# Which weight tiles the second stage decodes in which unit: three and then one, or two throughout

## Chip, cores and metric

The kernel runs on one core of a Trainium2 chip. The metric is the device time of one execution in microseconds (us). TensorE is called PE, VectorE DVE, ScalarE ACT, GpSimd POOL and SyncE SP here, as the profile calls them.

## What is computed

An attention layer, then two feed-forward layers over its 2304 rows of 512 values. The feed-forward weights are float64. The kernel splits each of their values, and the rows themselves, into a high and a low part in the float32 format, so that a product takes three matmuls (high by high, low by high, high by low).

```python
x = attention_with_memory(q, k, v, M_prev, z_prev, beta)   # (2304, 512)
h = x @ w_in                                               # 512 -> 2048
x = (h * tanh(softplus(h))) @ w_out                        # 2048 -> 512
a, b = x @ w1, x @ w2                                      # 512 -> 1024 each
out = ((a * b) @ w3) @ w_out2                              # 1024 -> 1024 -> 512
```

## The kernel before

**Stage one** is the attention, 16 pairs of heads. **Stage two** is the first feed-forward layer, and the change lies there. It takes the 2048 hidden columns in four quarters (`g`), and within a quarter eight units: four blocks of rows (`b`) by two halves of 288 rows (`z`). A unit runs 48 matmuls of `emit_h` (x by a quarter of `w_in`) and 48 of `emit_x2` (the activated result by a quarter of `w_out`), the latter for the unit before. `emit_x2` sums into PSUM banks of the tag X, of which there are three, and for each of its four column blocks DVE adds the bank to `x2` in SBUF (L575 in the first quarter, L577 later), which frees the bank for the block three further on. **The last stage** holds the second feed-forward layer; its `fold`, begun during the last quarter, multiplies `w3` by `w_out2` beforehand.

**Decoding.** A weight tile of 128x512 float64 values is turned into float32 pairs by `decode`: one load of 512 KB on SP's queue (L92), six DVE instructions (L98 to L104) and an addition on POOL (L105). Then one of two things follows:

- `split_w`, for the next quarter's weights (the generator `load_quarter(g + 1)`, eight tiles, called `nextq` in the loop): POOL rounds (L62) and subtracts (L65) into the tile `wqt`, and that is all. Such a tile is called N here.
- `split_to_dram`, for the weights of the last stage (the generator `predecode`, 24 tiles of `w1`, `w2` and `w_out2`, called `pre`): POOL rounds (L62) and subtracts (L120) in place, and two stores of 256 KB go out on SP's queue (L121, L122) to DRAM, from where the last stage reads them. Such a tile is called P here.

Both use the same buffers: `decoder(dk, 2, 2)` gives two for the raw load (`draw`) and two each for `da` and `de`. The next tile in a pair of `da` and `de` begins when POOL has subtracted, for an N, and when the stores have landed, for a P. Two P tiles are decoded during stage one, so 22 are left for stage two. The quarter after the present one needs its eight N tiles at its own start.

**What sets the order.** Each engine runs its instructions in a fixed order. A planner writes it when the program is built (`schedule_with_timeline_sim`): it takes an instruction of lower place in the source early when its own estimate of times says that the engine would be idle and the buffers are free. So where a step stands in the source is not just where it runs; once the order is written, an instruction that waits holds up all that stand behind it on its engine.

The loop of stage two, before: every unit asks for two steps of `nextq` (which has eight, so it is done after four units) and one step of `pre`.

Of the kernel before, what the change touches and what calls it, by code (L numbers as in the profile page):

```python
# [21 lines left out]
def fused_kernel(ctx: ExitStack, tc, q, k, v, M_prev, z_prev, beta, w_in, w_out, w1, w2, w3, w_out2, out):  # L22
# [47 lines left out]
    def steps(gen, n):  # L70

        for _ in range(n):
            next(gen, None)
# [9 lines left out]
    def decoder(stack, raw, n):  # L83
        dec.update(pool=stack.enter_context(tc.tile_pool(name="dec", bufs=1)), raw=raw, n=n)
# [54 lines left out]
    def predecode():  # L139
        for w, wd in ((w1, w1_dram), (w2, w2_dram), (w_out2, o2_dram)):  # L140
            for c in range(w.shape[0] // 128):
                for h in range(w.shape[1] // WN):
                    split_to_dram(wd[:, 128 * c:128 * c + 128, WN * h:WN * h + WN], words(w, 128 * c, WN * h))
                    yield
# [13 lines left out]
    def load_quarter(g):  # L158
        t = (wq if g % 2 == 0 else w2q[0]).tile([128, 2, KD + KQ, FQ], F32R, tag=f"wq{g % 2}", name="wqt")
        wts[g] = t  # L160
        for c in range(KD):
            split_w(t[:, 0, c], t[:, 1, c], words(w_in, 128 * c, FQ * g))
            yield
        for c in range(KQ):
            split_w(t[:, 0, KD + c], t[:, 1, KD + c], words(w_out, FQ * g + 128 * c, 0))
            yield
# [287 lines left out]
    def emit_h(u):  # L454

        g, b, z = u
        t = wts[g]
        x = xl[b]
        cs = slice(CH * z, CH * z + CH)
        y = [wps[0].tile([128, 2, CH], F32, tag=f"y{i}", name="y", bufs=1) for i in range(2)]  # L460
        hp = []
        for m in range(KQ):
            o = bank(HU.get(u, HT[g == NQ - 1])[m])[:, 0:CH]
            ms = slice(128 * m, 128 * m + 128)
            for kk in range(KD):
                mm(o, t[:, 0, kk, ms], x[:, 0, kk, cs], kk == 0, False)
                mm(o, t[:, 0, kk, ms], x[:, 1, kk, cs], False, False)
                mm(o, t[:, 1, kk, ms], x[:, 0, kk, cs], False, kk == KD - 1)
            hp.append(o)
        for m in range(KQ):  # L470
            nc.scalar.activation(out=y[m // 2][:, m % 2], in_=hp[m], func=AF.Tanh, scale=0.5)

        d = wps[0].tile([128, 1], F32, tag="dum", name="dum", bufs=2)
        first = nc.scalar.activation(out=d, in_=y[1][:, 1, 0:1], func=AF.Sin, scale=0.0)
        with tc.issue_after(first.ins):
            for i in range(2):
                nc.scalar.activation(out=y[i], in_=y[i], func=AF.Arctan, scale=-0.5, bias=half)
        gg = []
        for i in range(2):
            nc.scalar.activation(out=y[i], in_=y[i], func=AF.Sin, scale=-2.0, bias=halfpi)  # L480
            for j in range(2):
                nc.vector.tensor_tensor(out=y[i][:, j], in0=y[i][:, j], in1=hp[2 * i + j], op=ALU.mult)
            gh = wps[0].tile([128, 2, CH], F32R, tag="gh", name="gh", bufs=3)
            gl = wps[0].tile([128, 2, CH], F32R, tag="gl", name="gl", bufs=3)
            nc.scalar.copy(out=gh, in_=y[i])
            sub(gl, y[i], gh)
            gg.append((gh, gl))
        gt[u] = gg
# [9 lines left out]
    pre = predecode()  # L498
# [61 lines left out]
    def emit_x2(u):  # L560
        g, b, z = u
        t = wts[g]
        gg = gt.pop(u)
        c0 = S * b + CH * z
        for m in range(KD):
            o = psX()[:, 0:CH]
            ms = slice(128 * m, 128 * m + 128)
            for kk in range(KQ):
                gh, gl = (x[:, kk % 2] for x in gg[kk // 2])
                mm(o, t[:, 0, KD + kk, ms], gh, kk == 0, False)  # L570
                mm(o, t[:, 1, KD + kk, ms], gh, False, False)
                mm(o, t[:, 0, KD + kk, ms], gl, False, kk == KQ - 1)
            d = x2[:, m, c0:c0 + CH]
            if g == 0:
                nc.vector.tensor_copy(out=d, in_=o)  # L575
            else:
                nc.vector.tensor_tensor(out=d, in0=d, in1=o, op=ALU.add)  # L577
# [37 lines left out]
    def from_dram(t, d, cols):  # L615
        for i in range(2):
            dm(out=f(t[:, i]), in_=d[i, :, cols].rearrange("(k p) f -> p k f", p=128))

    def w_slot(s, name):
        return xp.tile([128, 2, KD, 512], F32R, tag=f"xs{s}", name=name, padded_shape=[128, 2, KD, S])  # L620

    folding = fold()
    nextq = iter(())
    prev = None
    w1t, w2t, wft = [None, None], [None, None], [None]
    for u in [(g, b, z) for g in range(NQ) for b in range(B) for z in range(2)]:
        g, b, z = u
        last = g == NQ - 1
        if u not in gt:
            if last and fpool[0] is None:  # L630
                steps(nextq, 100)
                steps(pre, 100)
                dk.close()
                fpool[0] = fk.enter_context(tc.tile_pool(name="fp", bufs=1))
                decoder(fk, 1, 2)
            emit_h(u)
        if last:
            if z == 0 and b > 0:
                wt, wd = ((w1t, w1_dram), (w2t, w2_dram))[(b - 1) % 2]
                i = (b - 1) // 2  # L640
                wt[i] = w_slot(b - 1, "w12t")
                from_dram(wt[i], wd, slice(512 * i, 512 * i + 512))
            if b > 0:
                steps(folding, 3)
        if prev is not None:
            emit_x2(prev)
        if not last:
            if b == 0 and z == 0:
                nextq = load_quarter(g + 1)
            steps(nextq, 2)  # L650
            steps(pre, 1)
        prev = u
    emit_x2(prev)
    w2t[1] = w_slot(3, "w12t")
# [101 lines left out]
```

## Time and profile before

| what | us |
|---|---|
| median of 3 runs (1074.55 to 1075.28) | 1075.14 |
| the profiled execution: its own time | 1075.49 |
| the profiled execution: span from first to last instruction | 1073.7 |
| PE busy | 1023.7 |
| DVE busy | 671.9 |
| POOL busy | 387.3 |

A busy time adds up the time in which an engine had an instruction running. For PE the ends are modelled and instructions overlap, so a busy PE need not be at its peak. Times of rows are counted from the start of the span.

### The profile page before, as it was taken

The page shows a single profiled execution, that of the slowest core. Times are in us where ns is not written, and L with a number is a line of the kernel's source. Part 1 is how long each engine was busy: PE and PEld are TensorE (multiplying, and loading weights), DVE is VectorE, ACT ScalarE, POOL GpSimd, SP SyncE. Part 2 cuts the span into 40 slices and gives each one's busy share as a digit, 9 for nine tenths or more (in the row PEclk, how much of TensorE's full clock was granted, in tenths as well). Part 3 has the DMA queues.
Part 4 walks back from the last instruction along what each step waited for, and adds up shares of the span by engine and source line. Part 5 has one row for each costly group of instructions (what it writes and reads, how often), then busy time and mean ns, then how long its engine had stood idle before and what let it go on. Part 6 is the DMA issues. An engine that isn't in the chain of part 4 may idle for free.

```text
span 1073.7 us, 19071 instructions
## 1 busy us (share of the span) xinstructions
PE 1023.7 (95%) x7128; PEld 913.2 (85%) x7128; DVE 671.9 (63%) x1563; ACT 548.0 (51%) x1157; POOL 387.3 (36%) x377
## 2 busy tenths in 40 slices
PE   6998898899998999999999999999999999999998
PEld 5665655567798999999999999999998999999997
DVE  6699999896689888888987535647551122222220
ACT  5776767677765666666666655653231222222221
POOL 7668898784255556555555001010100000000000
PEclk9999999999999999999999999999999999999999
DMA  6788777675233343333332264323115100000001
GB/s 149 167 188 188 186 181 184 169 187 117 79 98 101 112 161 109 109 130 127 118 99 101 63 243 146 136 89 128 62 58 176 40 5 17 20 21 16 6 20 40
DMA packets 111341, 116.70 MB, mean 109 GB/s; under 512 B 71696, under 2 KB 73744, under 8 KB 111248
## 3 DMA queue, kind: packets, MB, share of 16 engines
q1 hardware_dynamic: 111248, 115.48, 37.6%
q8 instruction: 56, 0.92, 0.4%
q14 instruction: 37, 0.30, 0.1%
HBM read 71.83 MB, written 21.50 MB: 87 GB/s over the span
## 4 chain that ended last, share of the span: by engine, by line
PE 62%; DVE 20%; POOL 7%; DMA 6%; issue 3%; SPq 1%; ACT 0%; DVEq 0%; POOLq 0%; ACTq 0%
PE psA L59 28%; PE psX L59 24%; PE psF L59 6%; DVE de L104 3%; POOL da L120 2%; DVE da L102 2%; PE psF L426 2%; DVE de L103 2%; DVE s L361 2%; DVE da L99 2%; POOL da L105 2%; DVE da L98 2%; DVE da L100 2%; DMA w_dram<-da 1%; DVE s L356 1%
## 5 line engine op out<-in xcount | busy, mean ns | idle before, releaser
L105 POOL TENSOR_TENSOR da<-da,de 128x512 f32<-128x512 f32 x72 | 100.1, 1395 | 336.0 <-DVE de L104 272.6
L59 PE MATMUL psX<-gh,wqt 128*128 128x288 f32 x1024 | 209.0, 298 | 9.9 <-DVE x L575 5.4
L59 PE MATMUL psA<-x2h,w12t 128*128 128x256 f32 x1152 | 210.4, 283 | 0.0
L59 PEld LDWEIGHTS psA<-x2h,w12t 128*128 128x128 f32 x1152 | 180.8, 192 | 1.0
L59 PEld LDWEIGHTS psX<-gh,wqt 128*128 128x128 f32 x1024 | 164.6, 188 | 13.5 <-DVE x L575 6.7
L59 PE MATMUL psA<-x2l,w12t 128*128 128x256 f32 x576 | 163.2, 284 | 0.4 <-DVE x2l L65 0.4
L59 PE MATMUL psX<-gl,wqt 128*128 128x288 f32 x512 | 150.9, 295 | 0.0
L686 DVE TENSOR_TENSOR bs<-bs,psA 128x256 f32<-128x256 f32 x72 | 30.3, 421 | 161.5 <-PE psA L59 156.8
L59 PE MATMUL psA<-xt,wqt 128*128 128x288 f32 x840 | 119.9, 296 | 0.0
L59 PEld LDWEIGHTS psA<-xt,wqt 128*128 128x128 f32 x840 | 115.0, 189 | 2.3 <-issue 1.0
L59 PEld LDWEIGHTS psA<-x2l,w12t 128*128 128x128 f32 x576 | 110.3, 192 | 1.4 <-DVE x2l L65 0.7
L366 ACT ACTIVATE s<-s,acc 128x512 f32<-128x512 f32 (+4 forms) x144 | 84.2, 587 | 39.7 <-DVE acc L361 34.2
L59 PE MATMUL psX<-wft,pbuf 128*128 128x512 f32 x432 | 101.7, 394 | 2.3 <-DMA wft<-w_dram 2.3
L59 PEld LDWEIGHTS psX<-wft,pbuf 128*128 128x128 f32 x432 | 81.4, 190 | 19.3 <-DMA wft<-w_dram 2.8
L59 PEld LDWEIGHTS psX<-gl,wqt 128*128 128x128 f32 x512 | 96.5, 189 | 0.2
L687 ACT CAST pbuf<-bs 128x256 fp32r<-128x256 f32 x72 | 29.3, 406 | 110.4 <-DVE bs L686 97.3
L98 DVE TENSOR_SCALAR da<-draw 128x512 int32<-128x512 int32 x72 | 44.1, 616 | 61.5 <-DMA draw<-in_moe_w_dram 23.1
L59 PE MATMUL psF<-xt,wqt 128*128 128x288 f32 x552 | 77.3, 295 | 0.0
L426 PE MATMUL psF<-ident,s 128*128 128x128 f32 x400 | 67.7, 283 | 10.0 <-DVE s L356 6.6
L59 PE MATMUL psX<-pt,raw 128*64 128x64 f32 (+4 forms) x576 | 74.8, 329 | 0.0
L59 PEld LDWEIGHTS psF<-xt,wqt 128*128 128x128 f32 x552 | 74.5, 188 | 0.1
L361 DVE CUSTOM_DVE_ANT_0 s<-psA,mask 128x512 f32<-128x512 f32 (+3 forms) x144 | 64.2, 477 | 15.0 <-PE psA L59 11.0
(116 smaller groups left out, 1920.8 us busy)
## 6 DMA issues: line engine op xcount, KB each, us to landing
draw<-in_moe_w_dram SPq DMA_DIRECT2D x32, 512.0 KB, 3.7
draw<-in_moe_w_out_dram SPq DMA_DIRECT2D x24, 512.0 KB, 3.9
draw<-in_moe_w_in_dram SPq DMA_DIRECT2D x16, 512.0 KB, 4.4
w12t<-w_dram SPq DMA_DIRECT2D x8, 1024.0 KB, 7.8
w_dram<-de SPq DMA_DIRECT2D x24, 256.0 KB, 2.4
w_dram<-da SPq DMA_DIRECT2D x24, 256.0 KB, 2.4
out_dram<-ob SPq DMA_DIRECT2D x18, 256.0 KB, 2.0
eqk<-hl SPq DMA_DIRECT2D x30, 144.0 KB, 2.7
```

Source lines behind the costliest of these rows:

```text
L59: nc.tensor.matmul(o, lhsT=l, rhs=r, start=start, stop=stop)
L98: V.tensor_scalar(out=ai, in0=hw, scalar1=0x7FFFFFFF, scalar2=None, op0=ALU.bitwise_and)
L99: V.tensor_scalar(out=a, in0=a, scalar1=2.0 ** -15, scalar2=122879.9921875, op0=ALU.max, op1=ALU.min)
L100: V.tensor_scalar(out=ai, in0=ai, scalar1=3, scalar2=0x3FFFFFF8, op0=ALU.logical_shift_left, op1=ALU.bitwise_and)
L102: V.scalar_tensor_tensor(out=ai, in0=hw, scalar=-0x40000000, in1=ai, op0=ALU.bitwise_and, op1=ALU.bitwise_or)
L104: V.scalar_tensor_tensor(out=e, in0=lw.bitcast(U32), scalar=2.0 ** -52, in1=e, op0=ALU.mult, op1=ALU.mult)
L105: nc.gpsimd.tensor_tensor(out=a, in0=a, in1=e, op=ALU.add)
L361: nc.vector.tensor_tensor_reduce(out=s, in0=o, in1=m, op0=ALU.add, op1=ALU.min, scale=-scale, scalar=init, accum_out=a,)
L366: nc.scalar.activation(out=s, in_=s, func=AF.Exp, scale=-1.0, bias=a, accum_out=r)
L426: nc.tensor.transpose(o[:, 128 * x:128 * x + 128], src[:, 128 * jb:128 * jb + 128], ident)
L686: nc.vector.tensor_tensor(out=bs, in0=bs, in1=pa, op=ALU.mult)
L687: nc.scalar.copy(out=t[:, 0, m], in_=bs)
```

## The change

In the first four units of a quarter (`b` is 0 or 1) the loop asks for two steps of `nextq` and none of `pre`; in the other four for two of `pre`. The 100 in place of the 2 takes whatever is left of `nextq` there, which is nothing. The number of tiles and the instructions of each stay the same; the 22 P tiles are asked for by the unit (2,3,0), the seventh of the third quarter, where it was the sixth.

```diff
         if not last:
             if b == 0 and z == 0:
                 nextq = load_quarter(g + 1)
-            steps(nextq, 2)
-            steps(pre, 1)
+            first_half = b < 2
+            steps(nextq, 2 if first_half else 100)
+            steps(pre, 0 if first_half else 2)
         prev = u
```

## Rows read from the trace of the kernel before

**Rows 1.** The page: busy time of PE and DVE; the chain that ended last.

```profile
PE 1023.7 (95%) x7128; PEld 913.2 (85%) x7128; DVE 671.9 (63%) x1563; ACT 548.0 (51%) x1157; POOL 387.3 (36%) x377
PE 62%; DVE 20%; POOL 7%; DMA 6%; issue 3%; SPq 1%; ACT 0%; DVEq 0%; POOLq 0%; ACTq 0%
```

**Rows 2.** Windows over the first three quarters: stretch, length, then each engine's busy time.

```profile
305.44:398.70 93.26, 88.52 (x659) 87.66 (x660) 81.71 (x154) 59.12 (x93) 49.37 (x42) 1.00 0.37 122
399.25:503.48 104.23, 103.02 (x768) 102.15 (x768) 89.90 (x176) 67.19 (x104) 57.70 (x49) 1.00 0.36 122
503.64:606.00 102.36, 99.30 (x730) 98.60 (x731) 82.64 (x163) 62.61 (x97) 51.93 (x44) 0.98 0.32 104
```

**Rows 3.** Timeline of PE: start, length, instruction, [idle before, releaser].

```profile
330.86 0.54 PE L59 MATMUL psX<-gh,wqt 128*128 128x288 f32 x2 [0.84 <-DVE x L575]
345.84 0.54 PE L59 MATMUL psX<-gh,wqt 128*128 128x288 f32 x2 [2.30 <-DVE x L575]
373.21 0.53 PE L59 MATMUL psX<-gh,wqt 128*128 128x288 f32 x2 [1.59 <-DVE x L575]
477.51 0.54 PE L59 MATMUL psX<-gh,wqt 128*128 128x288 f32 x2 [1.15 <-DVE x L577]
503.64 0.54 PE L59 MATMUL psX<-gh,wqt 128*128 128x288 f32 x2 [0.16 <-DVE x L577]
581.70 0.54 PE L59 MATMUL psX<-gh,wqt 128*128 128x288 f32 x2 [0.91 <-DVE x L577]
596.81 0.53 PE L59 MATMUL psX<-gh,wqt 128*128 128x288 f32 x2 [2.06 <-DVE x L577]
```

**Rows 4.** Windows of line 98 alone, a half quarter each: DVE busy (count).

```profile
399.25:451.40 52.15, 6.30 (x8) 1.00 0.34 112
451.40:503.50 52.10, 4.48 (x8) 1.00 0.39 132
```

**Rows 5.** The chain that ended last, in order of time: start, length, piece.

```profile
468.49 2.78 DMA w_dram<-da
...
482.21 2.00 DMA w_dram<-da
...
496.26 1.99 DMA o_dram<-da
```

**Rows 6.** Timeline of DVE, second quarter: start, length, instruction.

```profile
437.37 0.44 DVE L577 TENSOR_TENSOR x<-x,psX 128x288 f32<-128x288 f32 x1
...
449.90 0.44 DVE L577 TENSOR_TENSOR x<-x,psX 128x288 f32<-128x288 f32 x1
...
461.78 0.45 DVE L577 TENSOR_TENSOR x<-x,psX 128x288 f32<-128x288 f32 x1
...
474.67 1.41 DVE L103 TENSOR_SCALAR de<-da 128x512 int32<-128x512 int32 x1
...
477.02 0.44 DVE L577 TENSOR_TENSOR x<-x,psX 128x288 f32<-128x288 f32 x1
...
490.00 0.44 DVE L577 TENSOR_TENSOR x<-x,psX 128x288 f32<-128x288 f32 x1
...
501.26 0.76 DVE L103 TENSOR_SCALAR de<-da 128x512 int32<-128x512 int32 x2
...
503.13 0.45 DVE L577 TENSOR_TENSOR x<-x,psX 128x288 f32<-128x288 f32 x1
```

**Rows 7.** Timeline of DVE at the start of the first and of the second quarter.

```profile
304.94 0.44 DVE L575 COPY x<-psX 128x288 f32<-128x288 f32 x1
...
310.85 0.43 DVE L98 TENSOR_SCALAR da<-draw 128x512 int32<-128x512 int32 x1 [1.43 <-DMA w_dram<-da]
...
323.57 1.51 DVE L98 TENSOR_SCALAR da<-draw 128x512 int32<-128x512 int32 x1
...
411.61 0.44 DVE L577 TENSOR_TENSOR x<-x,psX 128x288 f32<-128x288 f32 x1
...
428.44 1.49 DVE L98 TENSOR_SCALAR da<-draw 128x512 int32<-128x512 int32 x1 [0.84 <-POOL wqt L65]
```

**Rows 8.** Windows around the start of the last quarter: the share before DMA is the granted clock.

```profile
597.00:600.00 3.00, 3.00 (x16) 3.00 (x16) 1.58 (x5) 1.35 (x2) 0.80 (x1) 0.60 0.56 175
600.00:603.00 3.00, 3.00 (x21) 3.00 (x21) 2.92 (x7) 1.70 (x2) 0.00 (x0) 0.84 0.00 0
603.00:606.00 3.00, 3.00 (x25) 3.00 (x25) 2.06 (x4) 0.82 (x2) 0.76 (x1) 1.00 0.01 3
```

## Prediction

> **What bounds the kernel now.** I read the page first. PE is busy for 95% of the span, yet only 62% of the chain that ended last is PE; 20% is DVE, 7% POOL and 6% DMA [rows 1]. So somewhere PE waits for a loop through those three. I then cut stage two into quarters. PE idles 4.7 us of the first (93.26 less 88.52), 1.2 us of the second and 3.1 us of the third [rows 2]; the second, least disturbed quarter gives PE's own price of a unit, 103.02 / 8 = 12.88 us. All the change can give back is in those 9 us, under 1% of the time.
>
> The timeline of PE shows where they are [rows 3]. Each stall is of one kind: the matmul that needs a bank of tag X waits for DVE's addition to `x2`. That addition depends on nothing slow; it stands behind a pair of decodes in DVE's fixed order, and the decodes are late. Two stalls, 0.84 and 2.30 us, fall in the third and fourth unit of the first quarter. One falls in the sixth unit of every quarter: 1.59, 1.15 and 0.91 us. A tail of 0.16 us follows two units later in the second quarter. The last, 2.06 us, stands at the end of the third quarter, where `w3` is loaded for the first time.
>
> Next, who decodes what and when. The source asks for three tiles a unit in a half and then one, but DVE doesn't run it so: line 98, the first instruction of each decode, runs eight times in the first half of the second quarter and eight times in the other [rows 4]. The planner has levelled the count already. What differs is the kind. Following the loads and stores, the pairs of a quarter run in the order NN, NP, NP, NN, NP, NP, PP, PP: two P tiles in the first half, six in the second.
>
> Why are pairs late? There are two buffers, so a pair can't begin before the pair ahead has given them back. An N gives its buffer back when POOL has subtracted, a P only when its store has landed, 2.0 to 2.8 us later [rows 5]. The first addition to `x2` of each unit stands right behind a pair, so its spacing is the length of the loop: 12.53, 11.88, 15.24, 12.98 and 13.13 us in the second half of the second quarter [rows 6]. The first two begin behind an NN and an NP pair and are under PE's 12.88. The 15.24 begins behind an NP pair whose P was last on POOL, and leads to a PP pair: that is the stall of 1.15 us. The last two begin behind PP pairs and are just above 12.88. So this loop and PE run neck and neck.
>
> **The change, part by part.** It removes and adds no instruction. PE and ACT have the same work, DVE the same 276 decode instructions in stage two (46 tiles by six), POOL the same 138, SP the same loads and stores. By count, then, nothing; all is in the order. If the planner keeps its habit of a pair a unit, a quarter becomes NN, NN, NN, NN, PP, PP, PP, PP, and two P tiles move from the first half to the second. With a moved P go its load and two stores on SP's queue, past the N loads. SP's queue holds six such issues more in a half quarter of 52 us, and nothing behind them is urgent.
>
> *The first quarter's early stalls.* Here the second pair held a P, and the third pair's first instruction waited 1.43 us for that store [rows 7]. The fourth pair starts 18.63 us after the first addition (323.57 less 304.94), against 16.83 in the second quarter, which has no stall there [rows 7]. With N tiles alone this lag of 1.8 us should go: the whole 0.84 and 0.96 of the 2.30. Bounds: nothing, if the crowded DVE makes the lag, and 3.14, if both stalls go. I take -1.8.
>
> *The sixth unit's stall.* No NP pair is left, so the 15.24 us loop as such is gone. With the tail this removes 1.59 + 1.15 + 0.91 + 0.16 = 3.81 us, to be set against what follows.
>
> *PP behind PP.* Loops that begin with a PP pair number 4, 4 and 3 in the three quarters. Each costs what it is above 12.88. The trace has two in this quarter, 12.98 and 13.13, a mean of 13.06: +0.18 each. The nearest other loop that ends with a P's store is the 15.24; the mean of the three is 13.78: +0.90 each. The pieces move as much: the store takes 2.00 or 2.78 [rows 5], and a decode instruction takes 0.38 us where POOL is idle (0.76 for two) and 1.41 where POOL works [rows 6]. Between 0.18 and 0.90 I take 0.48, a little under the middle: 11 by 0.48 = 5.3. Against it, DVE comes to this half ahead. It gained 0.35 + 1.00 = 1.35 us on PE in the two units before the stall [rows 6], and four NN pairs should do as well; I count half of it, as that gain was followed by the worst loop: 0.68 by 3 = 2.0. Net +3.3, bounds 0 (11 by 0.18, less 2.0) and 7.9 (11 by 0.90, less 2.0).
>
> The Trainium skill has a rule for the slow instruction ("SBUF — State Buffer", section "Who interferes with whom"): VectorE and GpSimd share a pair of ports as an exclusive lock, and whoever begins first blocks the other for the whole instruction. The trace agrees: 1.41 beside 0.38 us. By it, PP pairs in strict turn, decoding while POOL waits for them, are at the low price, and the sum would be -1.8 - 3.81 + 0 = -5.6 us instead of the -2.3 below.
>
> *The end of stage two.* The last P tiles are asked for one unit later. The number of pairs in that quarter is still seven, and the buffers set the pace, so I leave the 2.06 us as it is. After that stall the granted clock is 0.60 and 0.84 for two windows of 3 us, a mix of 2.4 and 1.2 GHz, and PE does 16 and 21 matmuls in them against 25 [rows 8]: 13 matmuls, at 3.00 / 25 = 0.12 us, are 1.6 us more. The stall's full price is 3.7 us.
>
> *Cover.* The eight N tiles are needed at the quarter's end and are done in its first half: no cost. The P tiles of `w_out2` are read only after PE has finished the third quarter.
>
> Sum: -1.8 - 3.81 + 3.3 = -2.3 us. The profiled execution took 1075.49 us, so it becomes 1073.2; the median is 0.35 below that execution, which gives 1072.8.
>
> **The rivals.** A measurement of this kernel tells about 0.2%, 2.15 us, from no change.
>
> *No change* (0.30). DVE runs two decodes a unit before and after [rows 4], the loop takes what it takes, and the stalls only change place: the early lag stays (0) and the PP loops cost the 3.8 us that the sixth units did. For it: levelled counts. Against it: the 15.24 has a cause that goes. Time 1075.1.
>
> *PP in a row is too long* (0.22, slower). Four PP pairs follow each other, each ending in a store that nothing overlaps. At 0.90 us a loop and with the early stalls unmoved the sum is -3.81 + 7.9 = +4.1: 1079.2; with the whole gain of 1.35 a quarter counted it is +2.0, 1077.2. It decides from 0.72 us a loop with the early stalls unmoved, from 0.89 with them reduced. For it: the 15.24 and the store of 2.78. Against it: 12.98 and 13.13 are the only loops of exactly this kind. The Trainium skill speaks for this rival ("DMA: Bandwidth & Descriptors", "Latency and other measured facts"): a transfer's fixed part grows with the load on HBM, and two P tiles a unit bring twice the stores. The trace leans the other way, with the 2.00 us store among the PP pairs.
>
> *The stall at the end of stage two goes* (0.08). If the planner, given the P tiles later, sets the first `w3` decode behind that unit's additions, 3.7 us go as well: -2.3 - 3.7 = -6.0, 1069.1. For it: the order there must be written anew. Against it: the same buffers and the same pairs.
>
> **How the numbers follow.** The forecast has 0.40, of which 0.32 is beyond the 0.2% and 0.08 within it; no change 0.30; slower 0.22; the last 0.08. So faster 0.32 + 0.08 = 0.40, same 0.38, slower 0.22. The range leaves out the lower tail of the last rival and the upper of the slower one: 1069.0 to 1078.5. The forecast alone spans 1070.5 to 1074.0.
>
> **What would show it.** Right: stores of P tiles only in the second half of a quarter; no PE stall of over 1 us in the first quarter's third and fourth units; spacings of the first `x2` addition of 12.9 to 13.5 us through the PP units, without a 15 us one. Wrong: spacings of 13.7 or more there with a stall in each unit; stalls over 2 us, above all with a lower clock behind them; the early stalls in place though no P is near; or an order that still mixes N and P.

## The result: slower by 0.9%, and where the trace puts it

Six runs of the changed kernel have a median of 1082.76 us (1080.50 to 1086.81), against 1073.65 for six of the kernel before. The ratio is 1.0089, with a 95% interval of 1.0065 to 1.0114. So the change costs some 9 us, where 2.3 us of gain were forecast.

The page of the changed kernel, its span and busy time:

```profile
span 1085.0 us, 19073 instructions
...
PE 1030.4 (95%) x7128; PEld 919.4 (85%) x7128; DVE 673.6 (62%) x1563; ACT 547.8 (50%) x1157; POOL 384.8 (35%) x377
```

The work is the same as in [rows 1] (PE 7128 matmuls, DVE 1563 instructions, POOL 377), yet PE is busy 6.7 us longer. Already this says that some matmuls ran slower, besides those that waited. The span is 11.3 us longer than before. The first `x2` addition of stage two starts at 308.27, not at 304.94 [rows 7]: 3.3 us came before the change can act, in stage one, whose length differs by more than that among the experiments (302.4 to 310.1). From that addition to the 24th unit's (619.06 here, 608.16 before) it is 310.79 against 303.22: stage two itself is 7.6 us longer. The last stage gives 0.4.

The timeline of PE in stage two, its waits for DVE, as in [rows 3]:

```profile
308.77 0.53 PE L59 MATMUL psX<-gh,wqt 128*128 128x288 f32 x2 [0.62 <-DVE x L575]
319.70 0.40 PE L59 MATMUL psX<-gl,wqt 128*128 128x288 f32 x1 [0.58 <-DVE gl L65]
324.04 0.53 PE L59 MATMUL psX<-gh,wqt 128*128 128x288 f32 x2 [1.42 <-DVE x L575]
377.25 0.85 PE L59 MATMUL psX<-gh,wqt 128*128 128x288 f32 x2 [3.32 <-DVE x L575]
470.41 0.53 PE L59 MATMUL psX<-gh,wqt 128*128 128x288 f32 x2 [0.39 <-DVE x L577]
486.03 0.85 PE L59 MATMUL psX<-gh,wqt 128*128 128x288 f32 x2 [2.64 <-DVE x L577]
513.73 0.53 PE L59 MATMUL psX<-gh,wqt 128*128 128x288 f32 x2 [0.54 <-DVE x L577]
594.23 0.53 PE L59 MATMUL psX<-gh,wqt 128*128 128x288 f32 x2 [2.60 <-DVE x L577]
609.53 0.53 PE L59 MATMUL psX<-gh,wqt 128*128 128x288 f32 x2 [0.48 <-DVE x L577]
```

With one of 0.17 at 539.66 they add up to 12.8 us. (The one at 319.70 waits for `gl` of the activated result, not for a bank.) Before it was 9.8: the 9.0 of [rows 3], 0.62 at the first unit and 0.15 at the quarter's end. That is +3.0, too little for 7.6. Three waits stand out, one in each quarter, in the sixth unit as before but 2.6 to 3.3 us long instead of 0.9 to 1.6. What follows them is in the windows of 3 us behind each, as in [rows 8] (the share before DMA is the granted clock):

```profile
377.25:380.25 3.00, 3.00 (x12) 3.00 (x13) 3.00 (x7) 1.47 (x3) 3.00 (x3) 0.50 0.69 183
380.25:383.25 3.00, 3.00 (x15) 3.00 (x14) 0.94 (x3) 1.16 (x1) 1.55 (x2) 0.50 0.84 320
486.03:489.03 3.00, 3.00 (x12) 3.00 (x13) 3.00 (x7) 1.50 (x3) 3.00 (x4) 0.50 0.80 243
489.03:492.03 3.00, 3.00 (x24) 3.00 (x23) 1.88 (x3) 1.53 (x2) 2.67 (x2) 0.98 0.67 254
594.23:597.23 3.00, 3.00 (x15) 3.00 (x16) 3.00 (x7) 1.50 (x3) 3.00 (x4) 0.62 0.19 70
597.23:600.23 3.00, 3.00 (x20) 3.00 (x20) 1.89 (x3) 1.54 (x2) 2.67 (x2) 0.81 0.52 192
```

PE counts as busy for all 3.00 us but does 12 to 24 matmuls instead of 25. The granted clock is 0.50 in the first three windows, the lower of 2.4 and 1.2 GHz, and a mix of both in the others. At 0.12 us a matmul the missing ones are 23, 14 and 15 in the three pairs of windows (of 50 each), 52 in all: 6.2 us, against the 1.6 that the prediction read behind the stall at the end of stage two [rows 8]. That is +4.6. With the +3.0 of the waits it makes 7.6, which is what stage two shows between these two executions.

More than half of these 7.6 us is clock, but that is no price of the change. The profiled execution is the slowest of the six, with a granted clock of 0.983 over its span. Three others had 0.992 and took 1080.50, 1081.92 and 1083.17 us, while nine runs of the kernel before that had 0.992 too, taken beside the experiments, have a median of 1073.68 (1072.19 to 1077.91). So at the same clock the change still costs some 8 us. The lower clock stands in part where PE would wait otherwise. The kernel with the new order in the later quarters alone (below) runs DVE and POOL through the third quarter in the same order, and there the clock stayed at 1.00 behind the sixth unit's wait:

```profile
592.01 0.40 PE L59 MATMUL psX<-gh,wqt 128*128 128x288 f32 x1 [2.38 <-DVE x L577]
607.40 0.40 PE L59 MATMUL psX<-gh,wqt 128*128 128x288 f32 x1 [2.07 <-DVE x L577]
```

```profile
592.01:595.01 3.00, 3.00 (x22) 3.00 (x23) 3.00 (x7) 1.50 (x3) 3.00 (x4) 1.00 0.19 71
```

PE did its matmuls at full speed and then waited 2.07 us, where the changed kernel, with the lower clock, waited 0.48. From the sixth unit's first `x2` addition to the seventh's it was 15.39 us there and 15.30 here: the loop of DVE, POOL and the stores sets the time, and the clock hardly adds to it.

Why the loop is long is seen on the engines. The timeline of DVE in the second quarter (each `x2` addition shown is the first of its unit), then of POOL:

```profile
456.47 0.44 DVE L577 TENSOR_TENSOR x<-x,psX 128x288 f32<-128x288 f32 x1
...
469.91 0.45 DVE L577 TENSOR_TENSOR x<-x,psX 128x288 f32<-128x288 f32 x1
...
479.23 0.43 DVE L98 TENSOR_SCALAR da<-draw 128x512 int32<-128x512 int32 x1 [4.77 <-issue]
...
483.98 1.63 DVE L104 SCALAR_TENSOR_TENSOR de<-draw,de 128x512 f32<-128x512 uint32 x1
485.53 0.44 DVE L577 TENSOR_TENSOR x<-x,psX 128x288 f32<-128x288 f32 x1
...
499.36 0.44 DVE L577 TENSOR_TENSOR x<-x,psX 128x288 f32<-128x288 f32 x1
...
513.23 0.44 DVE L577 TENSOR_TENSOR x<-x,psX 128x288 f32<-128x288 f32 x1
```

```profile
469.52 2.87 POOL L105 TENSOR_TENSOR da<-da,de 128x512 f32<-128x512 f32 x2 [6.85 <-DVE de L104]
472.37 2.21 POOL L62 TENSOR_SCALAR de<-da 128x512 fp32r<-128x512 f32 x2
474.55 2.54 POOL L120 TENSOR_TENSOR da<-da,de 128x512 fp32r<-128x512 f32 x2
483.74 1.32 POOL L105 TENSOR_TENSOR da<-da,de 128x512 f32<-128x512 f32 x1 [6.65 <-DVE de L104]
485.74 1.28 POOL L105 TENSOR_TENSOR da<-da,de 128x512 f32<-128x512 f32 x1 [0.68 <-POOL da L105]
```

From one addition to the next the loop runs through one engine after the other: POOL works on both P tiles until 477.09 (7.18 us after 469.91), then neither works until DVE begins the next pair at 479.23 (2.14), then DVE decodes until 485.53 (6.30), one of its instructions 1.63 us long because POOL has begun again. Together 15.62, against PE's 12.88. The trace names no releaser for the 2.14. The first tile's last store, issued at 475.87, took 3.3 us to land and so landed just before 479.23, and DVE can't begin a tile before that. Behind this loop the two tiles of a pair run one after the other (POOL's additions at 483.74 and 485.74, each x1), and the loops are 13.83 and 13.87. The issues of the stores from 300 to 620 us, before and then after, with the median from issue to landing:

```profile
w_dram<-de SPq DMA_DIRECT2D x14, 256.0 KB, 2.5
w_dram<-da SPq DMA_DIRECT2D x14, 256.0 KB, 2.5
```

```profile
w_dram<-de SPq DMA_DIRECT2D x14, 256.0 KB, 3.7
w_dram<-da SPq DMA_DIRECT2D x14, 256.0 KB, 2.9
```

So the stores became slower too, by 0.4 us for `da`, the later one of each tile. That is the direction of the rule that I had put beside the rival, that a transfer's fixed part grows with the load on HBM (the Trainium skill, "DMA: Bandwidth & Descriptors", "Latency and other measured facts"). Whether the load on HBM is the reason isn't shown, since the stores of two tiles are now under way together.

### The profile page after: what moved, and what is told of

It is laid out like the page before. It is cut to its first block, busy times and chain, and to the rows that moved or that the text cites. A ratio compares the mean times of both kernels' runs of the same rounds, so it can differ in the third digit from the quotient of the medians.

```text
span 1085.0 us, 19073 instructions
## 1 busy us (share of the span) xinstructions
PE 1030.4 (95%) x7128; PEld 919.4 (85%) x7128; DVE 673.6 (62%) x1563; ACT 547.8 (50%) x1157; POOL 384.8 (35%) x377
## 4 chain that ended last, share of the span: by engine, by line
PE 61%; DVE 22%; POOL 6%; DMA 5%; issue 5%; SPq 1%; ACT 0%; DVEq 0%; POOLq 0%; ACTq 0%
PE psA L59 28%; PE psX L59 24%; PE psF L59 5%; DVE de L104 3%; POOL da L120 3%; PE psF L426 2%; DVE de L103 2%; DVE s L361 2%; DVE da L102 2%; DVE da L98 2%; DVE s L356 2%; DVE da L99 2%; DVE da L100 1%; POOL de L62 1%; PE psX L262 1%
## 5 line engine op out<-in xcount | busy, mean ns | idle before, releaser
L59 PE MATMUL psX<-gh,wqt 128*128 128x288 f32 x1024 | 211.7, 300 | 12.4 <-DVE x L577 6.8
L98 DVE TENSOR_SCALAR da<-draw 128x512 int32<-128x512 int32 x72 | 41.0, 570 | 65.7 <-DMA draw<-in_moe_w_dram 21.3
```

Source lines behind the costliest of these rows:

```text
L59: nc.tensor.matmul(o, lhsT=l, rhs=r, start=start, stop=stop)
L98: V.tensor_scalar(out=ai, in0=hw, scalar1=0x7FFFFFFF, scalar2=None, op0=ALU.bitwise_and)
```

## Experiments

Unless said, each edit is made in the changed kernel, and the ratio is to the kernel before on the same chip, with its 95% interval.

**The change in one quarter, and in the others.** Two kernels keep the old order in part.

```diff
+            changed = g == 0        # the other kernel: g > 0
-            steps(nextq, 2 if first_half else 100)
-            steps(pre, 0 if first_half else 2)
+            steps(nextq, 2 if first_half or not changed else 100)
+            steps(pre, (0 if first_half else 2) if changed else 1)
```

> The new order in the first quarter alone; the other two keep the old one. Theory A (four P pairs in a row make a loop longer than PE's unit; DVE's fixed order hands it to PE as a stall, and a stall of over 2 us brings the half clock): the first quarter loses about 3 us, from the stall of 3.3 us in its sixth unit and the slow clock behind it, less the early stalls that go; total 3 to 4 us slower than before. Rival B (the loss comes from the later quarters, where P tiles of the next quarter's end pile up): no change within 1 us.

Measured: 0.9991 (0.9970 to 1.0012), no difference: a miss of theory A, and the time that rival B named. The long stall of the sixth unit did come, 2.88 us, but the first eight units took 106.7 us as before. The window behind that stall:

```profile
371.88:374.88 3.00, 3.00 (x22) 3.00 (x23) 3.00 (x7) 1.46 (x3) 3.00 (x3) 1.00 0.72 197
```

Here the clock stayed at 1.00, so a stall of over 2 us doesn't always bring the lower one. The waits of the quarter sum to 5.6 us against 5.5 before: what the early stalls gave back, the later one took. In the changed kernel the same quarter, with the same order of instructions on PE and DVE, took 109.1 us with waits of 5.9; the 2.5 us more are the clock's for the most part.

> The new order in the second and third quarters alone. Theory A: the stalls of 2.6 us in both and their slow clock stay, the stall where w3 is first loaded goes; 4 to 6 us slower than before, and this and the first-quarter kernel add up to the whole loss of 9. Rival C (the loss is a shift of the whole stage that any new order of the planner brings): each of the two kernels shows the whole loss or none.

Measured: 1.0065 (1.0032 to 1.0098), some 7 us. As expected in kind: stalls of 2.77, 2.38 and 2.07 us, the first and the last with half clock behind them, the 2.38 without. Units 8 to 23 took 202.9 us against 196.6. In this profile the old stall of the first quarter, 2.31 us here and 2.30 before [rows 3], also had half clock behind it, which it hadn't before: 1.4 us in the first eight units. The two kernels together make up some 6 of the 9 us; their intervals are too wide to say that a part is missing.

**Stores that hold no buffer.** The two stores of a P tile read another tile that is ready, so that `da` and `de` come back when POOL is done; in one kernel everywhere, in one in the later quarters (with the old order in the first), and in one on the kernel before.

```diff
     def split_to_dram(...):
         ...
+        if dec["n"] == 2:           # the second kernel: and dec.get("free"), set for g > 0
+            e = a = f(xl[0][:, 0, 0, 0:WN])
```

> The changed kernel, but in stage two the stores of the P tiles read a tile of x that is long ready, so da and de come back when POOL is done, not when the store has landed; as many bytes are stored, and the last stage multiplies by other values (its weights are not the right ones). Theory A with the landing as the cause: each P loop is 2.0 to 2.3 us shorter, 13.8 becomes 11.6, under PE's 12.88; no stall over 1 us in the second half of a quarter; 8 us or more faster than the changed kernel, at or under the kernel before. Rival D (the traffic of two P tiles a unit is the cause): the traffic is the same, so the time stays within 2 us of the changed kernel. Rival E (POOL's order, both tiles' steps in turn, is the cause): less than half comes back.

Measured: 1.0048 (1.0028 to 1.0067), half of the loss back, not all. In the PP halves no stall exceeded 0.9 us and most loops took 13.3 us (12.35 to 14.31 in the second quarter). But the planner, which sees buffers come free earlier, wrote the first quarter anew, with stalls of 3.07 us, where the changed kernel has 1.42, and of 1.61, where it has none. So this total doesn't isolate the landing.

> The second and third quarters in the new order, as before, but there the stores read a tile of x that is ready and hold no decode buffer (the last stage then multiplies by other values). The first quarter is that of the kernel before. Theory A (the exposed landing of the P stores): the 7 us that this order cost in those quarters come back, the time is within 2 us of the kernel before, and no stall of over 1 us is left in the units with P pairs. Rival F (two like tiles in a unit keep DVE and POOL from working at the same time, landing or no landing): 4 us or more of the 7 stay.

Measured: 1.0044 (1.0019 to 1.0068). The first quarter was again written anew, with a stall of 3.99 us. Units 8 to 23, where both have the changed order, can be compared: 195.7 us against 202.9 in the kernel of the later quarters above, and 196.6 before. Two of the four waits in the second quarter's PP units, in the timeline of PE:

```profile
482.37 0.53 PE L59 MATMUL psX<-gh,wqt 128*128 128x288 f32 x2 [0.34 <-DVE x L579]
495.69 0.53 PE L59 MATMUL psX<-gh,wqt 128*128 128x288 f32 x2 [0.26 <-DVE x L579]
```

The long stall is gone and the loops are 13.31 to 13.32 each. In those quarters the hold of the stores is the loss: 7 us come back when nothing waits for a landing, though the planner also changed DVE's order in the PP units. It doesn't bring the loop under PE's unit.

> The kernel before with stores that hold nothing in stage two (other values again). Theory A: its sixth-unit stalls of 0.9 to 1.6 us have the same cause and go; 2 to 4 us faster than the kernel before. Rival F: no change within 1 us.

Measured: 1.0058 (1.0037 to 1.0079), a miss. The sixth units' stalls shrank to 0.33 us at most (one of 0.86 us came in the unit behind, in the second quarter), but the first quarter got stalls of 3.06 and 1.62, as in the first of these three. This total by itself tells nothing of the landing.

Set side by side, the three do. With free stores the changed kernel and the kernel before run DVE in the same order, and from the first unit's addition to the 24th's they take 305.52 and 305.42 us, each loop alike within 0.03, although one has its P tiles in a row and the other mixes them. Units 8 to 23 take 195.9 us in both and 195.7 in the kernel between them; with stores that hold their buffers they take 196.6 in the old order and 201.7 in the new. So in these units all that the new order costs comes through the buffers that the stores hold, be it as a wait or in the order that the planner writes for it.

**POOL in strict order of tiles.** The addition of a tile is issued only after the last POOL step of the tile ahead.

```diff
+        with ExitStack() as turn:
+            if dec.get("depth") and dec.get("last") is not None:
+                turn.enter_context(tc.issue_after(dec["last"]))
+            nc.gpsimd.tensor_tensor(out=a, in0=a, in1=e, op=ALU.add)
```

> The changed kernel, but in stage two POOL finishes one tile (add, round, subtract) before it begins the next, where the planner took both adds, both rounds, both subtracts. The first buffer of a pair comes back some 2.5 us earlier, the second at the same time. Rival E (POOL's order is the cause): the P loops fall under 13 us and 5 us or more come back. Theory A with the landing of the second tile as the cause: the second tile's store lands as late as before, so the stalls shrink by under 1 us each and less than 3 us come back.

Measured: 1.0166 (1.0137 to 1.0194), the wrong way. In the second quarter 27 of 96 decode instructions of DVE took over 0.8 us and all of them 70.3 us, against 13 and 54.9 in the changed kernel. Now one tile is decoded while POOL works on the other, and both engines pay.

**One tile of each kind in a unit**, in one order and in the other.

```diff
-            steps(nextq, 2 if first_half else 100)
-            steps(pre, 0 if first_half else 2)
+            steps(nextq, 1)         # the other kernel: these two lines swapped
+            steps(pre, 1)
```

> One N and then one P in every unit. Theory A: each P's landing runs beside its partner's work in POOL and DVE, so no run of P pairs forms; the stalls are those of the kernel before or fewer; 1074 or less, unless the last N tiles come too late for the next quarter, which would show as a stall at its first unit. Rival G (what counts is that a quarter's P tiles are many or few in a half, by DMA traffic): the same, so only the place of the stalls tells.

Measured: 1.0124 (1.0081 to 1.0167), a miss, and no better than the change: seven stalls of 0.9 to 4.0 us.

> One P and then one N in every unit. Theory A: POOL takes the P first, its store lands while POOL works on the N, so this is the order with the least exposed landing: 2 us or more faster than N first, and 3 us or more faster than the kernel before. If the order within a pair doesn't count, both are equal within 1 us.

Measured: 0.9962 (0.9942 to 0.9982), faster than both kernels. Only the order of two lines differs between these two. Here 5 of the 96 decode instructions of the second quarter were slow, against 16 there, and no stall exceeded 1.73 us.

**Like pairs in turn, and P in the first half.**

```diff
+            steps(pre, 2 * (1 - z))     # the other kernel: steps(pre, 2 if first_half else 0)
+            steps(nextq, 2 * z)         #                   steps(nextq, 0 if first_half else 2)
```

> Two P in one unit, two N in the next, in turn: as many P pairs as in the changed kernel, but none behind another. Theory A1 (each P pair lengthens its loop by the landing, whatever comes next; the clock makes it dear): the stalls add up to much the same 12 us, but none is over 2 us, and no half clock follows; 3 to 5 us slower than the kernel before instead of 9. Theory A2 (only P behind P hurts, an N pair behind it takes the delay up): within 2 us of the kernel before or faster. Rival H (a pair of one kind always hurts, by DVE and POOL in turn): as slow as the changed kernel.

Measured: 1.0103 (1.0074 to 1.0132), as slow as the change, which rival H had said. The spacing alternates between some 14.4 and 12 us; 14 stalls of 0.3 to 1.85 us sum to 15.8. So PP pairs cost without standing in a row, and a short loop behind each long one doesn't pay it back. Two half-clock stretches followed stalls of no more than 1.75 and 1.85 us.

> The halves exchanged: the P pairs in the first four units of a quarter, the N pairs in the other four. Theory A: the run of P pairs counts, not its place; 6 to 11 us slower than the kernel before, with 15 us loops and half clocks now in the first half. Rival I (the run hurts because it meets the turn of the quarter, where the next quarter's first N tiles wait for PE to leave the old weights): 3 us or less slower.

Measured: 1.0007 (0.9991 to 1.0024), a miss by 6 us and more, and the time that rival I named. The run of P pairs isn't harmless away from the turn of the quarter: the second quarter was 3.1 us longer than before, with PP loops of 15.17, 13.83 and 13.89, but the first was 1.4 shorter and the 2.06 us at the end of stage two [rows 3] went. I take it that no P tile stood in the way of `w3` any more; that was not tried, and how much the turn of the quarter adds stays open.

**The order on POOL.** One P and one N a unit, P first, and N's rounding held back until P's subtraction has been issued.

```diff
     def split_w(...):
         ...
+        with ExitStack() as turn:
+            if dec["n"] == 2 and dec.get("last") is not None:
+                turn.enter_context(tc.issue_after(dec["last"]))   # P's subtraction
+            pool_round(hi, a)
         ...
+            steps(pre, 1)
+            steps(nextq, 1)
```

> One P, then one N in every unit, and POOL begins to round the N only when it has finished the P, so that the P's store always lands beside the N's work on POOL. Theory A: no stall over 1 us inside a quarter; at or under the kernel with P first (4 us faster than the kernel before), by up to 2 us. If it is slower than that one, the landing is not what the order within a pair changes.

Measured: 0.9907 (0.9890 to 0.9925), 1064.26 us: some 10 us faster than before, and by the two ratios some 19 faster than the change. The timeline of PE has two waits of over 0.4 us in stage two, one in the first quarter and one just behind it:

```profile
368.08 0.53 PE L59 MATMUL psX<-gh,wqt 128*128 128x288 f32 x2 [0.79 <-DVE x L578]
407.65 0.53 PE L59 MATMUL psX<-gh,wqt 128*128 128x288 f32 x2 [0.99 <-DVE x L580]
```

One loop of it, on POOL and then on DVE (L123 is P's subtraction, L65 is N's, L580 the addition to `x2`):

```profile
468.34 2.94 POOL L105 TENSOR_TENSOR da<-da,de 128x512 f32<-128x512 f32 x2 [4.51 <-DVE de L104]
471.95 1.30 POOL L123 TENSOR_TENSOR da<-da,de 128x512 fp32r<-128x512 f32 x1
474.43 1.69 POOL L65 TENSOR_TENSOR wqt<-da,wqt 128x512 fp32r<-128x512 f32 x1
480.63 2.94 POOL L105 TENSOR_TENSOR da<-da,de 128x512 f32<-128x512 f32 x2 [4.51 <-DVE de L104]
```

```profile
468.79 0.44 DVE L580 TENSOR_TENSOR x<-x,psX 128x288 f32<-128x288 f32 x1
...
475.42 1.32 DVE L98 TENSOR_SCALAR da<-draw 128x512 int32<-128x512 int32 x2
476.66 0.75 DVE L99 TENSOR_SCALAR da<-da 128x512 f32<-128x512 f32 x2
...
479.88 1.28 DVE L104 SCALAR_TENSOR_TENSOR de<-draw,de 128x512 f32<-128x512 uint32 x2
481.30 0.45 DVE L580 TENSOR_TENSOR x<-x,psX 128x288 f32<-128x288 f32 x1
...
487.91 1.19 DVE L98 TENSOR_SCALAR da<-draw 128x512 int32<-128x512 int32 x2 [0.22 <-DMA o_dram<-da]
```

P's subtraction ends at 473.25, and POOL goes on with N until 476.12, while the store lands; in the next loop DVE waits 0.22 us for it, at 487.91, and that is all that shows of the landing. Both buffers are back at nearly the same time, so DVE decodes both tiles in one go from 475.42 to 481.16 (x2 at 0.75 or 1.28 for two) while POOL rests for 4.51. The loop is 12.51 us, and PE sets it. Covering the landing is not all of it: with stores that hold nothing most loops took 13.3 us and DVE's 96 decode instructions of the second quarter 59.4 us, against 45.4 here, where POOL rests while DVE decodes.

**Two counter-tests.** POOL in order of tiles in the changed kernel, with either kind held back at its rounding; and the mirror of the kernel above, N first, with P's rounding held back.

```diff
     # the first: around pool_round in split_w and in split_to_dram
+            if dec["n"] == 2 and dec.get("last") is not None:
+                turn.enter_context(tc.issue_after(dec["last"]))
     # the second: the same in split_to_dram alone, and in the loop
+            steps(nextq, 1)
+            steps(pre, 1)
```

> The changed kernel with its N and P in separate halves, and on POOL the same rule as in the fast kernel: a tile's rounding begins only when the tile before it is finished (the additions stay free). Theory K (it is the mixing that counts: a P beside an N, so that the landing and the other tile's work run side by side): P beside P still has no partner for its landing; 4 us or more slower than the kernel before. Theory L (it is POOL's order alone, one tile at a time): at or under the kernel before, near 1064.

Measured: 1.0103 (1.0078 to 1.0127), no better than the change. An order on POOL alone doesn't help like pairs: theory L falls.

> One N and then one P in every unit, with P's rounding behind the N's last step on POOL, so that N and P alternate there as in the fast kernel, only the other one first in the unit. Theory K: what counts is the strict alternation, not who is first; within 3 us of the fast kernel (1064 beside 1075 before). Theory M (P must come first in the unit): 8 us or more slower than that one, as it was without the rule on POOL.

Measured: 1.0222 (1.0190 to 1.0255), the slowest of all, though it alternates as strictly as the fastest. So alternation alone (theory K) isn't the cause either, and P must be the first (M). The timelines of DVE and POOL show what goes wrong:

```profile
447.97 1.37 DVE L99 TENSOR_SCALAR da<-da 128x512 f32<-128x512 f32 x1
...
450.12 1.66 DVE L102 SCALAR_TENSOR_TENSOR da<-draw,da 128x512 int32<-128x512 int32 x1
```

```profile
447.68 1.38 POOL L105 TENSOR_TENSOR da<-da,de 128x512 f32<-128x512 f32 x1 [1.09 <-DVE de L104]
...
449.90 1.33 POOL L123 TENSOR_TENSOR da<-da,de 128x512 fp32r<-128x512 f32 x1
```

N's buffer is back early and P's late, so the two tiles fall out of step; DVE then decodes one while POOL works on the other, and its instructions that overlap POOL's take 1.37 to 1.66 us instead of 0.42 to 0.69. In the second quarter 19 of 96 are slow. In both cases shown POOL's instruction began first, and DVE's ended 0.28 and 0.55 us behind it. That agrees with the rule cited in the prediction (the Trainium skill, "SBUF — State Buffer", "Who interferes with whom": whoever begins first blocks the other for the whole instruction).

## Why the prediction was wrong

**The order** was forecast rightly. SP's stores of P tiles stand only in the second halves, the quarters run NN four times and PP four times, and no loop begins behind an NP pair.

**The early stalls of the first quarter** (-1.8 forecast). Both went, 0.84 and 2.30 [rows 3], as forecast and more. But the second unit, whose first `x2` addition came 15.27 us behind the first unit's instead of 11.93, got waits of 0.58 and 1.42 in their place, which the sum had at nothing. Net -1.1.

**PP behind PP** is the step that failed. I took 0.48 us a loop above 12.88. In the second quarter the four loops that begin behind a PP pair are 13.44, 15.62, 13.83 and 13.87, a mean of 14.19: +1.31. (All eleven have a mean of 14.26, with lower clock in some.) That is past the 0.72 to 0.89 from which the prediction's own slower rival decides. The 15 us loop, which I took to belong to the NP pair and to go with it, came back as the loop between the second PP pair and the third. I had averaged it with 12.98 and 13.13 as though they were samples of one thing. Its parts are 7.18 on POOL, 2.14 for the landing and 6.30 on DVE, one behind the other, where the sum took a mean excess. The 15.24 before had the same parts: 6.68 on POOL (to 468.46), 2.94 until DVE took up the second tile at 471.40, and 5.62 on DVE. That a PP pair would run in step like that pair, and not like the two at 12.98 and 13.13, was not to be read from it.

**What stood in the trace before.** The prediction takes 12.98 and 13.13 for the only loops of their kind. Behind PP pairs the trace also has 12.91 and 13.12 in the first quarter and 15.11 in the third (from 581.20 to 596.31), which ends at the stall of 2.06; the five exceed 12.88 by 0.57 on the mean. It also shows what order within a mixed pair is worth. In stage two before, six loops begin behind a pair whose P was first on POOL and take 11.3 to 12.4 us; five begin behind a pair whose P was last and take 14.4 to 15.2. Two that stand next to each other in [rows 6] are 11.88 (from 449.90) and 15.24 (from 461.78); POOL's subtractions in them (L120 for P, L65 for N):

```profile
452.55 1.81 POOL L120 TENSOR_TENSOR da<-da,de 128x512 fp32r<-128x512 f32 x1
454.33 1.28 POOL L65 TENSOR_TENSOR wqt<-da,wqt 128x512 fp32r<-128x512 f32 x1
...
465.92 1.29 POOL L65 TENSOR_TENSOR wqt<-da,wqt 128x512 fp32r<-128x512 f32 x1
467.17 1.29 POOL L120 TENSOR_TENSOR da<-da,de 128x512 fp32r<-128x512 f32 x1
```

So behind mixed pairs the long loop went with a P that came last, not with the mixture as such. A PP pair ends with a P too, though the four loops of 12.91 to 13.13 show that it need not be long.

**The lead from four NN pairs** (-2.0 forecast) wasn't there. The spacings behind the last three NN pairs are 13.21, 12.50 and 13.34, a mean of 13.0, and PE waits 0.39 us right behind the second PP pair, at 470.41.

**The price of a stall** lacked the clock. I had read a lower clock behind the 2.06 us stall [rows 8] and given it a price there, 1.6 us, but put none on the stalls that the slower rival would bring. With it the bound of 7.9 for the PP loops would have reached further, though less far than by its full price, since the next wait can be shorter for it (0.48 beside 2.07). The mark was named, though: stalls over 2 us with a lower clock behind them. Both came.

**The end of stage two.** I left its 2.06 us as it was; the wait at that place became 0.48. This didn't pay, since the 0.91 two units ahead of it became 2.60, and the half clock came behind that one.

**PE's own unit price** was nearly right. The best kernel's first additions stand 12.27, 12.51 and 12.72 us apart where PE never waits, but fewer than a unit's 96 matmuls stand in the first two. By the windows PE does 393 matmuls there in the 52.00 us from 443.00, 0.132 us each, so that a unit takes some 12.7 us, against the 12.88 read. That kernel's stage two, 293.7 us to the 24th unit, is 9.5 shorter than before, about the 9 us that the prediction took for all there was to gain.

**Rivals.** "PP in a row is too long", at 0.22, is what happened: +7.6 in stage two, where it was priced at +2.0 to +4.1. Its time of 1077 to 1079 was too low because a loop cost more than the 0.90 us that it used, and by the lower clock. "In a row" was the wrong word in it, since PP pairs in turn with NN pairs cost as much. The range, which ended at 1078.5, didn't hold the time.

**What stays open.** How much of the longer loop comes from the stores' slower landing, and how much from nothing running beside it, wasn't separated. The first quarter is written differently by the planner whenever a buffer's return moves, so the kernels with free stores and the one with P first compare more than one thing there. And which stall is followed by half clock isn't told by its length: 2.88 and 2.38 us were not, 1.75 and 1.85 were, and the first quarter's old stall was in one kernel (2.31) and was not in another (2.30).

## What to carry to other kernels

Before pricing a loop that shares two buffers between two engines and a store, add up its pieces in series from single rows, and ask for each pair what neither engine does while the store lands; an average over loops of different kinds hides it. Where one of two tiles gives its buffer back late, issue that tile first and let the other's work cover the landing, so that both return together: among kernels with the same instructions this order alone was worth the step from 1.0222 to 0.9907. And when a stall of a saturated TensorE is followed by a lower clock, don't add that whole price to the waits of one execution: the next wait may be shorter for it, as 0.48 us instead of 2.07 here. Compare runs at the same granted clock first.

## What the hardware showed that I had not expected

The stalls of 3.32 and 2.64 us were followed by a granted clock of 0.50: 12 matmuls in the 3 us behind 377.25 and 486.03, against 25 at 1.00. Yet where a loop of other engines set the pace, in the third quarter, this hardly showed in the time: 15.30 us with it, 15.39 without.

The overlap of DVE's and POOL's instructions sets more than one instruction's length. The same 96 decode instructions of a quarter take DVE 45.4 us in the best kernel and 63.2 in its mirror, a difference of 17.8 us that comes from the order of two tiles.
